# Part of a weight matrix loaded onto half of the partitions, in eight loads of eight partitions each

## The chip, the cores and the metric

The kernel runs on one core of a Trainium2 chip. The metric is device time in microseconds (us), the median of several executions. The profile is of one execution. Its span leaves out 1.5 to 1.9 us that the time includes.

Names used below: PE is TensorE, DVE is VectorE, SP is the queue that issues the loads. A "load" is one DMA from HBM into SBUF. A core has 16 DMA engines, and an ordinary load is divided over all 16 (the trace has 16 completion instants for each).

## The reference, cut to what matters

One token passes through an attention block with a cache of 65,536 positions and then through a gated feed-forward block. The change concerns the last product alone, `w_down` (3584 rows, 7.3 MB).

```python
def _B_ref(x, w_gate, w_up, w_down):          # x: 1 x 1024, F = 3584
    return _gelu(x @ w_gate) * (x @ w_up) @ w_down
...
h = _layernorm(x, axis=-1) * (1 + cb) + sb
x = x + gb * _B_ref(h, B_w_gate, B_w_up, B_w_down)
```

## The kernel before

All weights and the cache are streamed through ten SBUF slots by loads on the SP queue, mostly 2 MiB each. The product with a vector takes each 128x128 piece of the weights as the stationary operand and one column of the vector as the moving one, and waits for one load at a time. So PE works in bursts: it waits for a load, then does that load's matmuls.

```python
def matvec(bank, jobs, rhs, ready, nblk, pick=None, first=True):
    PE.wait(*ready)
    for (jb, view, k0, nk) in jobs:
        PE.wait(jb.tok)                      # this load has landed, on all its engines
        for kk in range(nk):
            for j in range(nblk):
                w = pick(view, kk, j) if pick else view[:, kk, j * P:(j + 1) * P]
                ins = pe.matmul(bank[:, j:j + 1], w, rhs[:, k0 + kk:k0 + kk + 1], ...)
        tok = PE.done(ins)
        release(jb, tok)                     # the slot may be loaded again
...
# w_down: row = (b * 128 + p) * 4 + e lies on partition p; 7 blocks b of 512 rows
wd_v = B_w_down.rearrange("(b p e) n -> p b e n", p=P, e=UE)
while b + 2 < NBF:                           # three loads of two blocks, 2 MiB each
    jb = plan_load(wd_v[:, b:b + 2, :, :], ...)
while b < NBF:                               # the last block as two loads of 512 KiB
    for e in range(0, UE, 2):
        jb = plan_load(wd_v[:, b, e:e + 2, :], flat(2, D), next(tail))
...                                          # (all cut)
v = matvec(acc_bank["dn"], j_d, u_col, (v_uc,), KD)
DVE.wait(v)
v = DVE.done(dve.tensor_tensor(t_dn, acc_bank["dn"], mod_sb[gb], ALU.mult))   # indices cut
# then y = t_dn + x1, a transpose on PE, and the store of 2 KB
```

`t_dn` is the first DVE instruction after the last matmul. Its start is a good mark for the end: what follows it (a sum, a transpose, a cast, a store) takes nearly the same time (2.7 to 2.8 us from its start to the end of the span).

## Time and profile before

| | before |
|---|---|
| time, median of 3 (range) | 444.28 us (444.15 to 444.35) |
| span of the profiled execution | 442.7 us |
| last up load landed on its last engine | 421.6 us |
| third 2 MiB down load, last engine | 436.8 us |
| last load, first and last engine | 433.8 and 439.2 us |
| `t_dn` starts | 439.90 us |

The first fence is from the page of the kernel before: the forty-slice view (busy tenths of the 16 DMA engines, then GB/s moved), the view of DMA queues (packets, MB, share of 16 engines' span), and the chain of waits that ended last.

```profile
DMA  8999999999999999999999999999999999999994
GB/s 329 429 423 426 434 431 426 429 427 421 432 429 432 426 427 437 432 429 428 434 434 430 429 429 433 431 434 429 429 434 431 432 429 428 423 424 424 427 425 177
...
q1 hardware_dynamic: 15328, 185.61, 98.5%
q8 instruction: 25, 0.41, 0.3%
...
DMA 75%; PE 20%; issue 2%; DVE 1%; SPq 1%; ACT 1%
```

The kernel is bound by the DMA engines: their loads (q1) keep them busy for 98.5% of the span. The small line q8: 25 packets of 16 KiB that bring instructions (instruction fetches). They run on the same DMA engines as the loads: one sets the loads of its engine back by 1.41 to 1.42 us (below).

The second fence is the timeline of PE and DVE in the last 20 us before the end: start and duration in us, engine, line, operation, output and inputs, how many, and in brackets the idle time ahead with what ended it.

```profile
421.68 2.03 PE L316 MATMUL kt_ps<-h_col,slot 128*128 128x1 bf16 x56 [2.25 <-DMA slot<-in_B_w_up_dram]
423.81 0.18 DVE L660 SCALAR_TENSOR_TENSOR u_col<-g,kt_ps 128x28 bf16<-128x28 f32 x1 [15.94 <-PE kt_ps L316]
...
426.74 1.84 PE L316 MATMUL kt_ps<-u_col,slot 128*128 128x1 bf16 x64 [3.03 <-DMA slot<-in_B_w_down_dram]
...
431.52 1.87 PE L316 MATMUL kt_ps<-u_col,slot 128*128 128x1 bf16 x64 [2.93 <-DMA slot<-in_B_w_down_dram]
...
436.83 2.29 PE L316 MATMUL kt_ps<-u_col,slot 128*128 128x1 bf16 x80 [3.45 <-DMA slot<-in_B_w_down_dram]
...
439.28 0.58 PE L316 MATMUL kt_ps<-u_col,slot 128*128 128x1 bf16 x16 [0.15 <-DMA slot<-in_B_w_down_dram]
439.90 0.17 DVE L664 TENSOR_TENSOR t_dn<-kt_ps,mod_sb 128x8 f32<-128x8 f32 x1 [15.91 <-PE kt_ps L316]
```

Each burst starts within 0.14 us of its load's landing. The third 2 MiB load (436.83) and the first 512 KiB load give one burst of 80 matmuls, and PE then waits only 0.15 us for the last load.

**Two finer readings of the trace.** They carry the argument, so here is how they are made.

- *Completion counts.* A load's semaphore rises by one for each DMA engine that has finished its share. The trace has these 16 instants for each load, so it shows how far apart the engines are.
- *Following the packets.* The trace has start, duration, size and queue of every packet, but not its engine. One engine's packets follow each other without a gap (the next one is recorded some 3 ns before the end of the last), and each engine has a known number of packets per load. Chaining the packets by these two rules gives 16 streams. It also shows which stream an instruction packet interrupts. Where two streams coincide to 2 ns, the chain may take one for the other.

These are the completion counts of the last load of before (us):

```
433.8 434.0 434.3 434.3 434.4 434.6 435.7 436.6 | 438.0 438.2 438.3 438.7 438.8 438.8 438.8 439.2
```

Eight engines are early, eight are 1.4 to 5.4 us behind them, and the gap is made by the instruction packets. Each takes 0.88 to 1.01 us on one engine, and that engine's loads are set back by more than that. An engine that meets none needs 4.90 us for its share of a 2 MiB down load. They go to eight engines in turn, as far as the chain can be followed.

### The profile page before, as it was taken

How to read it: one execution, taken by the hardware profiler on the slowest of the kernel's cores; microseconds unless marked ns; L12 is line 12 of the kernel's file. 1: busy time of each engine (PE TensorE's matmuls, PEld its weight loads, DVE VectorE, ACT ScalarE, POOL GpSimd, SP SyncE). 2: the span in 40 equal slices, each digit the busy share in tenths (PEclk: the TensorE clock that was granted, in tenths of full speed). 3: DMA queues.
4: the chain of work that ended last, by engine and by line, in shares of the span. 5: the costliest groups of instructions: out<-in, count | busy, mean ns of one | idle time of the engine just before them, and what ended most of it. 6: DMA issues, size and time to landing. Idle time of an engine off the chain costs nothing.

```text
span 442.7 us, 16779 instructions
## 1 busy us (share of the span) xinstructions
PE 335.0 (76%) x7849; PEld 325.2 (73%) x7849; DVE 164.8 (37%) x282; ACT 143.1 (32%) x548; POOL 3.8 (1%) x21
## 2 busy tenths in 40 slices
PE   1333468898979899989899988979898974654434
PEld 1333458898979899979799987969898964654434
DVE  1000046544536445544644644554544443210000
ACT  1000013444444333634533453543343562000000
POOL 2000000000000000000000000000000000000000
PEclk9999999867788956967955996895967785555555
DMA  8999999999999999999999999999999999999994
GB/s 329 429 423 426 434 431 426 429 427 421 432 429 432 426 427 437 432 429 428 434 434 430 429 429 433 431 434 429 429 434 431 432 429 428 423 424 424 427 425 177
DMA packets 15392, 186.08 MB, mean 420 GB/s; under 512 B 1536, under 2 KB 1536, under 8 KB 3840
## 3 DMA queue, kind: packets, MB, share of 16 engines
q1 hardware_dynamic: 15328, 185.61, 98.5%
q8 instruction: 25, 0.41, 0.3%
q14 instruction: 7, 0.06, 0.0%
q10 hardware_dynamic: 32, 0.00, 0.0%
HBM read 185.60 MB, written 0.00 MB: 419 GB/s over the span
## 4 chain that ended last, share of the span: by engine, by line
DMA 75%; PE 20%; issue 2%; DVE 1%; SPq 1%; ACT 1%
DMA slot<-in_A_v_cache_dram 55%; PE kt_ps L417 9%; DMA slot<-in_A_wq_dram 8%; DMA slot<-in_B_w_up_dram 6%; DMA slot<-in_B_w_down_dram 6%; PE b L481 5%; PE sc_ps L437 3%; PE kt_ps L316 1%; SPq L212 1%; PE b L461 1%; ACT p_sb L547 1%; PE b L451 1%; DVE kt_sb L612 0%; PE b L621 0%; DVE zs L597 0%
## 5 line engine op out<-in xcount | busy, mean ns | idle before, releaser
L417 PE MATMUL kt_ps<-ident,slot 128*128 128x128 bf16 x2048 | 171.9, 252 | 4.9 <-DMA slot<-in_A_k_cache_dram 3.0
L516 DVE COPY kt_sb<-kt_ps 128x2048 bf16<-128x2048 bf16 x96 | 117.5, 1225 | 100.0 <-PE kt_ps L417 99.7
L417 PEld LDWEIGHTS kt_ps<-ident,slot 128*128 128x128 bf16 x2048 | 148.6, 114 | 6.6 <-issue 4.2
L516 ACT ACTIVATE kt_sb<-kt_ps 128x2048 bf16<-128x2048 bf16 x32 | 60.1, 1878 | 217.7 <-PE kt_ps L417 217.7
L481 PE MATMUL b<-p_sb,slot 128*128 128x8 bf16 x2048 | 71.0, 167 | 29.5 <-DMA slot<-in_A_v_cache_dram 20.9
L481 PEld LDWEIGHTS b<-p_sb,slot 128*128 128x128 bf16 x2048 | 65.1, 100 | 32.2 <-DMA slot<-in_A_v_cache_dram 22.2
L547 ACT ACTIVATE p_sb<-sc_ps,mneg 128x64 bf16<-128x64 f32 x256 | 83.6, 560 | 5.7 <-DVE mneg L542 5.7
L547 ACT ACTIVATION_READ_ACCUMULATOR p_sb<-sc_ps,mneg 128x1 f32 x256 | 77.2, 364 | 0.0
L437 PE MATMUL sc_ps<-q_buf,kt_sb 128*128 128x8 bf16 x2048 | 67.4, 167 | 0.1
L437 PEld LDWEIGHTS sc_ps<-q_buf,kt_sb 128*128 128x128 bf16 x2048 | 65.1, 100 | 0.2 <-issue 0.2
L316 PE MATMUL kt_ps<-h_col,slot 128*128 128x1 bf16 x448 | 16.2, 172 | 16.9 <-DMA slot<-in_B_w_up_dram 9.1
L316 PEld LDWEIGHTS kt_ps<-h_col,slot 128*128 128x128 bf16 x448 | 15.6, 118 | 17.6 <-DMA slot<-in_B_w_up_dram 9.4
L316 PE MATMUL sc_ps<-s_col,slot 128*128 128x1 bf16 x384 | 11.5, 165 | 15.8 <-DMA slot<-in_w_mod_dram 15.8
L535 DVE TENSOR_REDUCE m_col<-sc_ps 128x8 f32<-128x512 f32 x32 | 21.8, 681 | 4.4 <-PE sc_ps L437 4.4
L316 PEld LDWEIGHTS sc_ps<-s_col,slot 128*128 128x128 bf16 x384 | 11.0, 105 | 16.4 <-DMA slot<-in_w_mod_dram 16.4
L540 DVE TENSOR_REDUCE mg<-b 8x1 f32<-8x128 f32 x32 | 8.9, 279 | 34.4 <-PE b L451 34.4
L316 PE MATMUL sc_ps<-h_col,slot 128*128 128x1 bf16 x256 | 7.4, 165 | 12.6 <-DMA slot<-in_A_wq_dram 12.6
L316 PEld LDWEIGHTS sc_ps<-h_col,slot 128*128 128x128 bf16 x256 | 7.1, 104 | 12.9 <-DMA slot<-in_A_wq_dram 9.3
L461 PE MATMUL b<-negi,mg 8*128 8x8 f32 x64 | 15.0, 304 | 0.4 <-DVE mg L540 0.4
L461 PEld LDWEIGHTS b<-negi,mg 8*128 8x128 f32 x64 | 12.0, 233 | 2.6 <-DVE mg L540 0.6
L316 PE MATMUL kt_ps<-u_col,slot 128*128 128x1 bf16 x224 | 6.6, 165 | 9.6 <-DMA slot<-in_B_w_down_dram 9.6
L316 PEld LDWEIGHTS kt_ps<-u_col,slot 128*128 128x128 bf16 x224 | 6.3, 104 | 9.9 <-DMA slot<-in_B_w_down_dram 6.8
(74 smaller groups left out, 63.2 us busy)
## 6 DMA issues: line engine op xcount, KB each, us to landing
slot<-in_A_k_cache_dram SPq DMA_DIRECT2D x32, 2048.0 KB, 29.6
slot<-in_A_v_cache_dram SPq DMA_DIRECT2D x32, 2048.0 KB, 33.2
slot<-in_w_mod_dram SPq DMA_DIRECT2D x8, 1536.0 KB, 19.0
slot<-in_A_wq_dram SPq DMA_DIRECT2D x4, 2048.0 KB, 37.0
slot<-in_A_wo_dram SPq DMA_DIRECT2D x4, 2048.0 KB, 34.7
slot<-in_B_w_gate_dram SPq DMA_DIRECT2D x4, 1792.0 KB, 39.4
slot<-in_B_w_up_dram SPq DMA_DIRECT2D x4, 1792.0 KB, 29.0
slot<-in_B_w_down_dram SPq DMA_DIRECT2D x3, 2048.0 KB, 30.4
```

Of the source, the lines that this page charges most:

```text
L212: sp.dma_start(j.view, j.src).then_inc(j.tok[0], 16)
L316: ins = pe.matmul(bank[:, j:j + 1], w, rhs[:, k0 + kk:k0 + kk + 1], start=first, stop=True, skip_group_check=True,)
L417: ins = pe.transpose(kt_ps[:, half * 2048 + t * P:half * 2048 + (t + 1) * P], j_k[i].view[:, b * TB + t, :], ident[:, :],)
L437: ins = pe.matmul(sc_ps[:, base + n * REP:base + (n + 1) * REP], kt_sb[:, j % 2, n, :], q_buf[:, j % SITES, :], start=True, stop=True,)
L451: ins = pe.transpose(b6[0:REP, 32:32 + P], m_col[:, j % 2, :], identf[:, :]) if emit else None
L461: ins = pe.matmul(b6[:, 256:256 + REP], mg8[:, j % 2:j % 2 + 1].to_broadcast([REP, P]), negi[:, :], start=True, stop=True,)
L481: ins = pe.matmul(b7[:, s * REP:(s + 1) * REP], j_v[j].view[:, n, :], p_sb[:, s, n, :], start=(n == 0), stop=(n == CH - 1),)
L516: ev[i % SITES][b].done(act.activation(dst, src, ACT.Copy) if E_ is AC else dve.tensor_copy(dst, src))
L535: m1[s].done(dve.tensor_reduce(m_col[:, j % 2, :].unsqueeze(2), scv, AX.X, ALU.max))
L540: m2[s].done(dve.tensor_reduce(mg8[:, j % 2:j % 2 + 1], b6[0:REP, 32:32 + P], AX.X, ALU.max))
L547: ins = act.activation(p_sb[:, s, :, h], scv[:, h, :], ACT.Exp, bias=mneg[:, j, h:h + 1], scale=scale, accum_out=z_all[:, j, h:h + 1],)
```

## The change

The intent is to level the DMA engines. 256 rows of `w_down` (512 KiB) are put on partitions 0 to 63 alone, four rows per partition, and are loaded by eight loads of eight partitions, each four partitions apart. Such a load is divided over eight DMA engines, meant to be the early ones. The other 3328 rows are divided over all 16 as before. Call the eight loads the *low loads*; they come first, then three loads of 2 MiB, then two of 256 KiB (before: three of 2 MiB and two of 512 KiB).

```diff
+HP = 64
+    blocks = [(0, HP, UE), (HP * UE, P, UE // 2)]      # (first row, partitions, rows each)
+    while blocks[-1][0] + blocks[-1][1] * blocks[-1][2] < F:
+        blocks.append((blocks[-1][0] + blocks[-1][1] * blocks[-1][2], P, UE))
+    ucols = [(row0, n, e) for row0, _, n in blocks for e in range(n)]   # 30 columns, were 28
...
+        job.pieces = [(job.view[a], src[a]) for a in parts] if parts else [(job.view, src)]
...
-            sp.dma_start(j.view, j.src).then_inc(j.tok[0], 16)
+            for dst, src in j.pieces:
+                sp.dma_start(dst, src).then_inc(j.tok[0], 16)
...
+        low = [slice(a + t, a + 4 * 8, 4) for a in range(0, HP, 32) for t in range(4)]
+        jb = plan_load(wd_v[0], lambda t: flat(UE, D)(t)[0:HP], next(tail), parts=low)
+        j_d.append((jb, jb.view, ucol0[0], UE))
+        for b in range(2, len(blocks), 2):                 # three loads of 2 MiB
+            ...
+        for e in range(blocks[1][2]):                      # two loads of 256 KiB
+            jb = plan_load(wd_v[1][:, e:e + 1, :], flat(1, D), next(tail))
...
-                            bank[:, j:j + 1], w, rhs[:, k0 + kk:k0 + kk + 1],
+                            bank[:, j:j + 1], w, rhs[0:w.shape[0], k0 + kk:k0 + kk + 1],
```

(Cut to its core; the rest renames sizes.) Because the 64 partitions fill only half a column, the hidden vector needs 30 columns instead of 28: 32 more matmuls for gate and up, 16 more for down.

More of the change, by code (lines that the diff above doesn't have):

```diff
@@ L108, in bass_adaLN_cond__gqa_block_cached__geglu_ffn__decode_kernel @@
     assert FD % UE == 0 and M6 <= SLOT and KD % 2 == 0
+    blocks = [(0, HP, UE), (HP * UE, P, UE // 2)]
+    while blocks[-1][0] + blocks[-1][1] * blocks[-1][2] < F:
+        blocks.append((blocks[-1][0] + blocks[-1][1] * blocks[-1][2], P, UE))
+    assert blocks[-1][0] + P * UE == F and len(blocks) % 2 == 0
+    ucols = [(row0, n, e) for row0, _, n in blocks for e in range(n)]
+    ucol0 = [sum(n for _, _, n in blocks[:i]) for i in range(len(blocks))]
+    FU = len(ucols)
     SP = Eng(nc, nc.sync, "c_sp")
@@ L158, in bass_adaLN_cond__gqa_block_cached__geglu_ffn__decode_kernel @@
     Rmat = kt_sb[:, 0, 0:HQ * HQ // P, :].rearrange("p a b -> p (a b)").rearrange("p (a b) -> p a b", a=HQ)
-    g1 = sb("g1", [P, FD])
-    g2 = sb("g2", [P, FD])
-    g3 = sb("g3", [P, FD])
-    g4 = sb("g4", [P, FD])
-    gth = sb("gth", [P, FD])
-    u_col = sb("u_col", [P, FD], dt.bfloat16)
+    g1 = sb("g1", [P, FU])
+    g2 = sb("g2", [P, FU])
+    g3 = sb("g3", [P, FU])
+    g4 = sb("g4", [P, FU])
+    gth = sb("gth", [P, FU])
+    u_col = sb("u_col", [P, FU], dt.bfloat16)
     t_dn = sb("t_dn", [P, KD])
@@ L184, in bass_adaLN_cond__gqa_block_cached__geglu_ffn__decode_kernel, with plan_load @@
     loads = []
-    def plan_load(src, view_fn, slot, site=None):
+    def plan_load(src, view_fn, slot, site=None, parts=None):
         if site is not None:
@@ L191, in plan_load @@
         else:
-            nfill[slot] += 1
+            nfill[slot] += len(parts or (0,))
             tok = (fill[slot], 16 * nfill[slot])
         job = Job(view_fn(slots[slot]), tok, slot)
-        job.src = src
+        job.pieces = [(job.view[a], src[a]) for a in parts] if parts else [(job.view, src)]
         job.freed = None
@@ L233, in emit_all @@
         wu_v = B_w_up.rearrange("(k p) n -> p k n", p=P)
-        wd_v = B_w_down.rearrange("(b p e) n -> p b e n", p=P, e=UE)
+        wd_v = [B_w_down[r0:r0 + np_ * n, :].rearrange("(p e) d -> p e d", e=n) for r0, np_, n in blocks]
         kh = [A_k_cache[0, g].rearrange("(p n) d -> p n d", p=P) for g in range(Hkv)]
@@ L258, in emit_all @@
         j_d = []
-        NBF = FD // UE
-        b = 0
-        while b + 2 < NBF:
+        low = [slice(a + t, a + 4 * 8, 4) for a in range(0, HP, 32) for t in range(4)]
+        jb = plan_load(wd_v[0], lambda t: flat(UE, D)(t)[0:HP], next(tail), parts=low)
+        j_d.append((jb, jb.view, ucol0[0], UE))
+        for b in range(2, len(blocks), 2):
+            assert blocks[b][0] + P * UE == blocks[b + 1][0]
             jb = plan_load(
-                wd_v[:, b:b + 2, :, :],
+                B_w_down[blocks[b][0]:blocks[b][0] + 2 * P * UE, :].rearrange("(b p e) n -> p b e n", p=P, e=UE),
                 lambda t: t[:, 0:2 * UE * D].rearrange("p (b e n) -> p b e n", b=2, e=UE),
@@ L266, in emit_all @@
             )
-            j_d.append((jb, jb.view.rearrange("p b e n -> p (b e) n"), b * UE, 2 * UE))
-            b += 2
-        while b < NBF:
-            for e in range(0, UE, 2):
-                jb = plan_load(wd_v[:, b, e:e + 2, :], flat(2, D), next(tail))
-                j_d.append((jb, jb.view, b * UE + e, 2))
-            b += 1
+            j_d.append((jb, jb.view.rearrange("p b e n -> p (b e) n"), ucol0[b], 2 * UE))
+        for e in range(blocks[1][2]):
+            jb = plan_load(wd_v[1][:, e:e + 1, :], flat(1, D), next(tail))
+            j_d.append((jb, jb.view, ucol0[1] + e, 1))
         issue_ready()
@@ L639, in pick_gu @@
         def pick_gu(view, kk, j):
-            b, e = divmod(j, UE)
-            return view[:, kk, b * UE * P:(b + 1) * UE * P].rearrange("p (m e) -> p e m", e=UE)[:, e, :]
-        g = acc_bank["g"][:, 0:FD]
-        v_g = matvec(acc_bank["g"], with_view(j_g), h2_col, (v_h2,), FD, pick_gu)
+            row0, n, e = ucols[j]
+            return view[:, kk, row0:row0 + n * P].rearrange("p (m e) -> p e m", e=n)[:, e, :]
+        g = acc_bank["g"][:, 0:FU]
+        v_g = matvec(acc_bank["g"], with_view(j_g), h2_col, (v_h2,), FU, pick_gu)
         DVE.wait(v_g)
@@ L656, in emit_all @@
         v = DVE.done(dve.scalar_tensor_tensor(g2[:, :], gth[:, :], 1.0, g1[:, :], ALU.add, ALU.mult))
-        v_u = matvec(acc_bank["u"], with_view(j_u), h2_col, (v_h2,), FD, pick_gu)
+        v_u = matvec(acc_bank["u"], with_view(j_u), h2_col, (v_h2,), FU, pick_gu)
         DVE.wait(v, v_u)
         v_uc = DVE.done(
-            dve.scalar_tensor_tensor(u_col[:, :], g2[:, :], 0.5, acc_bank["u"][:, 0:FD], ALU.mult, ALU.mult)
+            dve.scalar_tensor_tensor(u_col[:, :], g2[:, :], 0.5, acc_bank["u"][:, 0:FU], ALU.mult, ALU.mult)
         )
```

## The prediction

> **What bounds the kernel now.** DMA. The forty-slice view has the 16 DMA engines at nine tenths in nearly every slice; the queue view gives the load queue 98.5% of their span; the chain of waits is 75% DMA. In the trace's packet records a 16 KiB packet takes 611 ns and an engine starts its next about 607 ns later: each engine runs at a fixed 27 GB/s, and the end is set by the engine with most work.
>
> The engines do not end together. Each load's completion count climbs by one per DMA engine, and the trace has these 16 instants. In the last load (512 KiB) they are 433.8, 434.0, 434.3, 434.3, 434.4, 434.6, 435.7, 436.6 us for eight engines and 438.0 to 439.2 for the others. After it come its 16 matmuls (to 439.86), result, transpose and store, to 442.7. The lag is made by instruction fetches: 25 packets of 16 KiB on the instruction queue, each 0.88 to 1.01 us on one engine. Following the packet times, each sets one engine back about 1.2 us, and only eight engines get them, in turn. The eight-partition loads of x and c (8 packets each) interleave with the other eight. [...]
>
> **What the change does.** [...] Late engines lose 32 KiB, 1.21 us; early ones gain 1.21 us[...]. Early ends become 435.1 to 437.9, late ones 436.8 to 438.0: nearly level. The last two loads shrink to 256 KiB. Added: 32 matmuls for gate and up (60 instead of 56 per load; 36 ns each) and 16 for down (28.6 ns each), mostly under loads; eight more DMA issues of about 0.35 us, ahead of need (the last load was issued near 416 us, moved from 432).
>
> **On the critical path.** The late engines carry the same bytes up to the third 2 MiB load, so that still lands at about 436.8 us. Before, 80 matmuls then ran to 439.12 and waited 0.15 us for the last load's 16. After, the two small loads land near 437.4 and 438.0, while PE needs until 436.83 + 2.29 = 439.12 for the 80 matmuls left. Of the 1.2 us that DMA gains, about 0.5 is lost to TensorE's tail: the end comes 0.7 us earlier.
>
> **Prediction: 443.6 us, range 442.9 to 444.4.** Faster by over 2%: 1%; within 2%: 98%; slower by over 2%: 1%.
>
> **What would show it.** The last load's final count near 438.0, its spread 2 to 3 us instead of 5.4; the third 2 MiB load still near 436.8; 80 down matmuls with no DMA wait before the last ones; t_dn near 439.2; the low loads landing before the last up load is consumed (about 424).
>
> **What would make it wrong.** The 48 extra matmuls move instruction fetches earlier: a fetch that now meets a late engine before 436.8 costs up to 1.2 us, and eats the gain. If the low loads use the late engines, the end is 1.2 us later (445). If eight small DMAs cost queue room, the last loads start late. A chip difference of a few tenths is of the gain's size.

In the prediction is a rule that numbers the engines of a small load, and a length for completion packets. The rule led from "interleave with the other eight" to low loads on the eight early engines, which would get 64 KiB each where all 16 had 32. The sum for the end: 1.2 us gained by DMA, less 0.5 for TensorE's tail, makes 0.7, and 444.3 becomes 443.6. Of the early ends, 435.1 to 437.9, a term is 0.1 us (433.8 and 436.6 plus 1.21 make 435.0 and 437.8); they are not in that sum. The completion packets take 9 ns in the traces.

## The result, and the profile after

The changed kernel took 445.44 us, median of five runs (445.11 to 446.96), against 444.28 us before (444.04 to 444.35). The ratio of times is 1.0035 with a 95% interval of 1.0023 to 1.0047. Ratios here are the mean time of one kernel's runs over that of the other's of the same rounds, so they are not quite the ratio of the medians quoted. So it is within 2%, but clearly slower, by 1.2 us, where a gain of 0.7 us had been predicted, and it lies outside the predicted range (442.9 to 444.4).

The page of the changed kernel, same views as above:

```profile
DMA  8999999999999999999999999999999999999993
GB/s 327 428 427 425 430 430 435 427 424 424 429 432 427 433 428 432 433 430 432 430 435 425 435 429 435 427 432 429 438 427 432 428 435 429 421 423 424 428 419 156
...
q1 hardware_dynamic: 15456, 185.61, 98.4%
q8 instruction: 25, 0.41, 0.3%
...
DMA 79%; PE 17%; issue 1%; ACT 1%; DVE 1%; SPq 1%
```

Nothing in the averages tells the two kernels apart: the same bytes, the same rate, as many instruction packets. The last slices differ, and the timeline shows them (L325 is the line that was L316):

```profile
421.96 2.13 PE L325 MATMUL kt_ps<-h_col,slot 128*128 128x1 bf16 x60 [2.17 <-DMA slot<-in_B_w_up_dram]
424.44 1.01 PE L325 MATMUL kt_ps<-u_col,slot 64*128 64x1 bf16 x32 [0.35 <-DVE u_col L669]
428.44 1.86 PE L325 MATMUL kt_ps<-u_col,slot 128*128 128x1 bf16 x64 [2.99 <-DMA slot<-in_B_w_down_dram]
433.33 1.86 PE L325 MATMUL kt_ps<-u_col,slot 128*128 128x1 bf16 x64 [3.03 <-DMA slot<-in_B_w_down_dram]
438.22 2.29 PE L325 MATMUL kt_ps<-u_col,slot 128*128 128x1 bf16 x80 [3.03 <-DMA slot<-in_B_w_down_dram]
...
440.55 0.17 DVE L673 TENSOR_TENSOR t_dn<-kt_ps,mod_sb 128x8 f32<-128x8 f32 x1 [16.17 <-PE kt_ps L325]
```

The first 2 MiB load lands at 428.44 instead of 426.74, and the third at 438.22 instead of 436.83. The 80 matmuls behind it run without a wait, as predicted, and set the end: `t_dn` at 440.55 instead of 439.90. So the loss is in the landing of the 2 MiB loads, which the prediction had left where they were.

The completion counts of the last load show who is late (us):

```
433.2 433.4 435.2 435.2 435.2 435.7 437.1 437.3 437.5 437.6 437.7 437.9 437.9 438.1 | 439.3 439.5
```

Fourteen engines are done by 438.1, as predicted for all 16. Two are more than 1 us behind them. Following the packets through the trace says which. Below, per stream: the instruction packets that met it from 352 us on (start, us), its low packets, and the start of its completion packets for the last up load and the last load (us; the count that PE sees is 0.3 to 0.5 us later).

```
changed kernel                                    before
fetches     low  last up   last load              fetches     last up   last load
-            8   416.30    434.79                 -           416.35    433.55
-            8   416.41    434.90                 -           416.47    433.67
-            8   416.45    434.94                 -           416.77    433.96
-            8   416.90    435.39                 -           416.77    433.96
-            8   418.29    436.77                 -           416.91    434.10
-            8   418.91    437.40                 -           417.03    434.23
396          8   420.63    439.12   <--           -           418.23    435.42
404          8   420.49    438.97   <--           -           419.10    436.30
-            0   416.83    432.82                 395         420.63    437.83   <--
-            0   417.06    433.06                 404         420.50    437.70   <--
428          0   419.83    437.24                 432         420.24    438.86
390          0   420.98    436.97                 389         420.86    438.05
421          0   420.18    437.59                 422         419.85    438.46
413          0   421.27    437.26                 413         421.23    438.43
371          0   421.59    437.59                 370         421.35    438.55
384          0   421.63    437.62                 383         421.29    438.49
```

The eight engines that move the low loads and the eight that get the instruction packets are not disjoint. They share two (marked; in this trace the fourth and the fifth of the round, though streams that coincided earlier may be swapped). Those two were late already and now carry 64 KiB of these rows where they had carried 32. And two early engines carry no low load and idle from 433.1 on.

The last instruction packet of each trace (437.6 and 439.4 us) is left out of the table: streams were ending or had ended then, so which one met it can't be told, and no load was set back by it. A second chaining had to give every stream whole loads in their order; it gives the same 16 streams for both kernels, and agrees with what is told of experiments 1 and 8.

### The profile page after: what moved, and what is told of

Read it like the earlier page. It is cut to its first block, busy times and chain, and to the rows that moved or that the text cites. A ratio compares the mean times of both kernels' runs of the same rounds, so it can differ in the third digit from the quotient of the medians.

```text
span 443.3 us, 16883 instructions
## 1 busy us (share of the span) xinstructions
PE 335.6 (76%) x7897; PEld 325.7 (73%) x7897; DVE 164.8 (37%) x282; ACT 143.2 (32%) x548; POOL 3.8 (1%) x21
## 4 chain that ended last, share of the span: by engine, by line
DMA 79%; PE 17%; issue 1%; ACT 1%; DVE 1%; SPq 1%
DMA slot<-in_A_v_cache_dram 52%; PE kt_ps L426 8%; DMA slot<-in_A_k_cache_dram 8%; DMA slot<-in_B_w_up_dram 8%; DMA slot<-in_B_w_down_dram 6%; DMA slot<-in_w_mod_dram 5%; PE b L490 4%; PE sc_ps L446 3%; PE kt_ps L325 1%; SPq L222 1%; ACT p_sb L556 1%; PE b L470 1%; PE b L460 0%; ACT kt_sb L525 0%; DVE kt_sb L525 0%
## 5 line engine op out<-in xcount | busy, mean ns | idle before, releaser
L325 PE MATMUL kt_ps<-h_col,slot 128*128 128x1 bf16 x480 | 17.1, 172 | 16.1 <-DMA slot<-in_B_w_up_dram 8.7
L325 PEld LDWEIGHTS kt_ps<-h_col,slot 128*128 128x128 bf16 x480 | 16.4, 117 | 16.8 <-DMA slot<-in_B_w_up_dram 9.0
L325 PE MATMUL sc_ps<-s_col,slot 128*128 128x1 bf16 x384 | 11.5, 165 | 16.1 <-DMA slot<-in_w_mod_dram 16.1
L325 PEld LDWEIGHTS sc_ps<-s_col,slot 128*128 128x128 bf16 x384 | 11.1, 105 | 16.7 <-DMA slot<-in_w_mod_dram 16.7
L325 PE MATMUL sc_ps<-h_col,slot 128*128 128x1 bf16 x256 | 7.5, 165 | 12.5 <-DMA slot<-in_A_wq_dram 12.5
L325 PEld LDWEIGHTS sc_ps<-h_col,slot 128*128 128x128 bf16 x256 | 7.1, 104 | 12.8 <-DMA slot<-in_A_wq_dram 9.3
L325 PE MATMUL kt_ps<-u_col,slot 128*128 128x1 bf16 (+1 forms) x240 | 7.0, 165 | 9.4 <-DMA slot<-in_B_w_down_dram 9.1
L325 PEld LDWEIGHTS kt_ps<-u_col,slot 128*128 128x128 bf16 (+1 forms) x240 | 6.7, 104 | 9.7 <-DMA slot<-in_B_w_down_dram 9.3
```

Source lines behind the costliest of these rows:

```text
L325: ins = pe.matmul(bank[:, j:j + 1], w, rhs[0:w.shape[0], k0 + kk:k0 + kk + 1], start=first, stop=True, skip_group_check=True,)
```

## The experiments

Three theories were put against each other. **A**: two of the engines that get instruction packets are among those that move the low loads. **B**: the 48 extra matmuls are more instructions, and bring an instruction packet that falls in a bad place. **C**: the eight small loads cost their engines time beyond their bytes.

### 1. The changed kernel again (label again)

No edit.

> The changed kernel once more, to see how its runs spread. Theory A (two of the eight engines that get the instruction fetches are among the eight that move the low loads): of the 16 counts of the first 2 MiB down load, less those of the last up load, two late engines again show 7.4 us and two early ones 4.9 us; the last load lands 439.3 to 439.5 us with two engines over 1 us behind the other six late ones. Time 445 to 447, over before by 0.8 to 2.7 us, with more spread than before's 0.3 us. Theory B (the 48 extra matmuls bring one more instruction fetch in time to delay one engine): one engine, not two, is behind, and which one changes.

Measured: 445.58 us median (445.3 to 446.0, four runs) against 444.18 before, ratio 1.0035 (1.0019 to 1.0052). The last load's counts end with 438.1, 438.2 | 439.5, 439.6: two engines behind. Following the packets gives the same picture as above: six low-load streams reach the end of the up loads between 416.3 and 418.5, and two, both interrupted by instruction packets, at 420.7. This agrees with A. B had one engine behind.

C falls with these traces too. A low-load stream goes from the completion of the up load to that of its eighth low load in 2.50 us (416.30 to 418.80), and eight packets of 8 KiB at 309 ns take 2.44 us once their overlap of some 3 ns is taken off. So a small load costs its engine about 7 ns beyond its bytes, and the six early ones among the eight are never last.

### 2. The low rows in one load over all engines (label all16)

```diff
-        low = [slice(a + t, a + 4 * 8, 4) for a in range(0, HP, 32) for t in range(4)]
+        low = None
```

> The low 256 rows in one DMA of 64 partitions, so over all 16 engines, 32 KiB each, as many bytes per engine as before; the extra matmuls, the split and the small last loads stay. Theory A: every late engine is as late as in before, the third 2 MiB load lands near 438.0 (436.8 and 1.2 us), the last load near 439.2 with a spread of 5.4 us, 80 matmuls follow from 438.0, t_dn near 440.4, time near 444.8: 0.4 to 0.6 over before, and under the changed kernel by 0.2 to 1 us. Theory B: the third 2 MiB load lands as late or later than in the changed kernel by another 1.2 us (439.4), time 446.5. Theory C (eight small DMAs cost time on their engines beyond their bytes): as A in time, but then the low-load engines of the changed kernel would all be late by the same, which its counts must show.

Measured: 449.34 us against 444.18 before, ratio 1.0118 (1.0101 to 1.0135). This missed all three expectations, those of A and C by 4.5 us and that of B by 2.8 us, because the experiment was not the clean control it was meant to be. The load of 64 partitions kept all 16 engines busy (DMA share 1.02 below), but from 422 to 426 us all its packets of 8 KiB are slow, with medians of 545 ns in the first two of these microseconds and 616 in the last two, instead of 309, and the up packets beside them are slowed too (481 instead of 272 ns). The windows view of 416 to 427 us, of this kernel and then of the changed one (busy time of each engine, granted clock, DMA share, GB/s), shows it in sum:

```profile
416.00:427.00 11.00, 4.27 (x120) 4.10 (x120) 0.16 (x1) 0.00 (x0) 0.00 (x0) 0.50 1.02 269
```

```profile
416.00:427.00 11.00, 5.27 (x152) 5.02 (x152) 0.18 (x1) 0.00 (x0) 0.00 (x0) 0.50 1.01 425
```

The engines are as busy (1.02), yet move 269 instead of 425 GB/s. So a full "busy" share does not mean full speed: the same packets take longer. What slows them is not shown; the trace shows only that they are slow. The change's own low loads, of eight partitions four apart, do not have this fault: in its trace, from 416 to 428 us, only one 8 KiB packet is over 309 ns (804, in the wake of an instruction packet). This run is 5.2 us over before, where experiment 5, whose first load has as many bytes on all 128 partitions, is 0.5 over. It says nothing on A against B.

### 3 and 4. Marking the engines (labels marks and marks2)

The trace has no engine numbers, but loads of few partitions use few engines (the 64 low packets of the changed kernel lie on eight streams, eight on each). The author assumed that a smaller load uses a part of the engines of a larger one. Then low loads of different sizes give each engine, or pair of engines, its own number of low packets: pairs of 13, 9, 6 and 4 in the first run, and 11, 11, 10, 8, 8, 6, 6 and 4 in the second.

```diff
-        low = [slice(a + t, a + 4 * 8, 4) for a in range(0, HP, 32) for t in range(4)]
+        low = [slice(t, 32, 4) for t in range(4)]                                # 4 of eight
+        low += [slice(32 + t, 32 + 4 * 6, 4) for t in (0, 1)]                    # 2 of six
+        low += [slice(34, 48, 4), slice(35, 48, 4), slice(50, 64, 4)]            # 3 of four
+        low += [slice(56, 64, 4), slice(57, 64, 4), slice(51, 56, 4), slice(59, 64, 4)]
```

> The same 64 partitions of low rows in loads of eight, six, four and two partitions (4, 2, 3 and 4 loads)[...]. Each packet with its completion is about 0.32 us, so the offsets between the counts of the last up load and of the first 2 MiB down load are 4.9 us plus 4.1, 2.9, 1.9, 1.3 and 0. Theory A: exactly two late engines show one of the offsets over 0, and its size tells which pair they belong to. If all eight late ones show 4.9 us, theory A is wrong. Time about 446 to 448, not of interest.

Measured: 445.94 us, one run. The packet counts that follow from the assumption came out: two streams each with 13, 9, 6 and 4 low packets, eight with none. Two late streams had low packets: one with 4, one with 6. Both had met instruction packets.

The second one splits the pairs (loads of eight, five, three, seven and two):

```diff
+        low = [slice(t, 32, 4) for t in range(4)]
+        low += [s for t in (0, 1) for s in (slice(32 + t, 52, 4), slice(52 + t, 64, 4))]
+        low += [slice(32 + t, 60, 4) for t in (2, 3)] + [slice(62, 64, 1)]
```

> The low partitions in loads of eight (4), five and three (2 of each), seven (2) and two (1)[...]. In the runs so far, following the packet times gave two engines that get instruction fetches and carry low packets, in the run of marks with 6 and 4 low packets[...]. Theory A expects two such engines again[...]. If no fetch engine carries low packets here, theory A is wrong.

Measured: 445.3 us, one run, on another chip. Again two streams with instruction packets (at 397 and 404) carry low loads. One has 6 low packets. Of the other, the chain follows three and loses the rest; 61 of the 64 low packets are assigned, so the three that remain are its own, which makes 6. The second chaining assigns all 64 and gives 6 to both, and 6 and 4 in the first run. On the same assumption an engine with 6 in the first run has 8 or 6 here, and one with 4 has 6 or 4, so six and six fits. Which engines of the core the two are is not shown; that two engines are in both sets is. A stands.

### 5. The order alone, no engine favoured (label even2)

The first 512 rows as two blocks of two rows on all 128 partitions. Order and small last loads stay, the extra matmuls go.

```diff
-    blocks = [(0, HP, UE), (HP * UE, P, UE // 2)]
+    blocks = [(0, P, UE // 2), (P * UE // 2, P, UE // 2)]
...
-        jb = plan_load(wd_v[0], lambda t: flat(UE, D)(t)[0:HP], next(tail), parts=low)
+        jb = plan_load(wd_v[0], flat(UE // 2, D), next(tail))
```

> The first 512 rows as two blocks of two rows on all 128 partitions: no engine gets more than another,[...] the matmuls are as many as before; the order and the two small last loads stay as in the changed kernel. Theory A and the tail of TensorE: third 2 MiB load at 438.0, last load at 439.2 with a spread of 5.4 us, 80 matmuls from 438.0 to 440.3, t_dn 440.4 (before 439.9), time 444.7 (+0.4 to +0.6). Theory B (the extra matmuls' fetches are the loss): like before, 444.2. Theory C (small DMAs): 443.6 to 444.2, as nothing small is left in front.

Measured: 444.52 us (444.39 to 444.58) against 444.05 before (443.89 to 444.14). The ratio 1.0011 has an interval that includes 1 (0.9994 to 1.0027), but the runs of the two do not overlap. Timeline of its end:

```profile
437.59 2.29 PE L324 MATMUL kt_ps<-u_col,slot 128*128 128x1 bf16 x80 [3.00 <-DMA slot<-in_B_w_down_dram]
...
439.92 0.17 DVE L672 TENSOR_TENSOR t_dn<-kt_ps,mod_sb 128x8 f32<-128x8 f32 x1 [16.06 <-PE kt_ps L324]
```

The last load landed at 438.8, but 80 matmuls from 437.59 on were still running, and `t_dn` came 1.1 us after the landing, where before needs 0.7 (439.2 to 439.90). By the medians the new order alone costs about 0.5 us. The trace offers a reason: 256 KiB land in 0.65 us each, less than PE needs to catch up with the 2 MiB load before them, so PE ends 0.4 us later after the landing. This is the term that the prediction called PE's tail, and its size fits. But the loss itself is not in this trace, whose `t_dn` is no later than that of before (439.92 and 439.90), because the landings were 0.4 us earlier; the traces vary by that much. That the order costs 0.5 us is thus likely and not proven.

### 6. PE's tail in the changed kernel (label after_split)

```diff
         for b in range(2, len(blocks), 2):
+            if b + 2 == len(blocks):                  # the third 2 MiB as two of 1 MiB
+                for bb in (b, b + 1):
+                    jb = plan_load(wd_v[bb], flat(UE, D), next(tail))
+                    j_d.append((jb, jb.view, ucol0[bb], UE))
+                continue
```

> The changed kernel with its third 2 MiB load cut into two of 1 MiB, so that TensorE has 48 instead of 80 matmuls left when the last big load lands. If TensorE's tail is worth what the trace says (32 matmuls, 0.9 us, less what the last load's own landing then limits): landings as in the changed kernel (438.2 for the last 1 MiB, 439.5 for the last load), t_dn 439.9 instead of 440.55, time 0.5 to 0.8 under the changed kernel, so 444.8 to 445.0. If the tail doesn't bound the end: no change, 445.5.

Measured: 444.59 us (444.44 to 444.69) against 444.05 before, ratio 1.0011 (0.9995 to 1.0028). It is 0.54 us over before, where the changed kernel was 1.2 and 1.4 us over before in its two sets of rounds, so the cut is worth 0.6 to 0.9 us by medians of different chips, and 0.4 us between the two traces.

```profile
438.42 1.67 PE L330 MATMUL kt_ps<-u_col,slot 128*128 128x1 bf16 x48 [1.43 <-DMA slot<-in_B_w_down_dram]
...
440.12 0.17 DVE L678 TENSOR_TENSOR t_dn<-kt_ps,mod_sb 128x8 f32<-128x8 f32 x1 [16.20 <-PE kt_ps L330]
```

The last big load lands as late as in the changed kernel (438.4), so the two overloaded engines are still there (last load: 437.6 | 439.3, 439.7), but 48 matmuls are left instead of 80, and `t_dn` starts at 440.12 instead of 440.55.

### 7 and 8. The same idea with engines that are all early (labels four and four_al)

128 rows, eight per partition, on partitions 0 to 15, in four loads of four partitions, meant for four early engines without the two shared ones (four streams carry these packets in experiment 8). The last 2 MiB load is cut as in 6. The expectation's figure for the last load, 438.6, is 439.2 less 0.6: the twelve other engines lose 16 KiB each, 0.6 us at the 607 ns that an engine takes for 16 KiB in before.

```diff
-HP = 64
+HP = 16
+LE = 8
...
+    blocks = [(0, HP, LE), (HP * LE, P, UE - HP * LE // P)]
...
+        low = [slice(t, HP, 4) for t in range(4)]
```

> The same idea with the two late engines left out: 128 rows, eight per partition, on partitions 0 to 15, in four loads of four partitions[...]; half the bytes; the last 2 MiB cut as above, then three small loads. Theory A:[...] no low-load engine is the last; last load 438.6, t_dn 439.0, time 443.4. But the 168 extra matmuls bring the next instruction fetch from 439 to about 432, which may set one late engine back by 1.2 us: last load 439.2 to 439.8, time 444.0 to 444.5. If the identity of the engines is not the cause, it is no better than the changed kernel with the same cut (444.9).

Measured: 448.53 us against 444.05, ratio 1.0101 (1.0085 to 1.0118), 3.6 us or more over every expectation. The cause is not in the last stage. Its last up load landed at 425.2 us, 3.6 us later than in before, and the packets were longer in all stages: 16 KiB packets took 615.9 ns on average from 60 to 340 us, against 612.0 in before, and 7 KiB packets 277.3 against 273.1 from 390 to 415 us. The edit had done one more thing. With 35 columns, the small tensors that are allocated ahead of the load slots need more room, and the slots began at byte 62,400 of a partition instead of 62,208. The first is 192 over a multiple of 256, the second is a multiple of 256. Two runs test that. The first repeats *four* with 64 bytes of padding (slots at 62,464, a multiple of 256):

```diff
     y_row = sb("y_row", [KD, P], dt.bfloat16)
+    pad = sb("pad", [P, 16])
```

> The kernel 'four' with 64 bytes of padding, so that the load slots begin at a multiple of 256 bytes again, as in before (in 'four' they began 192 bytes past one; its packets took 274 instead of 272 and 616 to 622 instead of 611 ns in all stages, and the last up load landed 3.6 us later than in before). If that is the cause: packets at 272 and 611 ns again, last up load near 421.6,[...] time 444.2 to 444.6; one engine over 1 us behind the rest by the fetch near 431.6, and no low-load engine last. If the loss came from loads of four engines: 448.

Measured: 444.74 us (444.37 to 444.84) against 444.18, ratio 1.0008 (0.9991 to 1.0025). The packets are back at 612.0 and 273.4 ns, and the last up load landed at 421.8. So the 3.8 us were the address. The version gains nothing over before, and its trace says why:

```profile
437.92 1.62 PE L332 MATMUL kt_ps<-u_col,slot 128*128 128x1 bf16 x48 [1.42 <-DMA slot<-in_B_w_down_dram]
439.78 0.38 PE L332 MATMUL kt_ps<-u_col,slot 128*128 128x1 bf16 x8 [0.24 <-DMA slot<-in_B_w_down_dram]
```

The last load's counts are 433.4 to 438.4 for 15 engines and 439.7 for one. The chain of packets finds four streams with four low packets each, none of them with an instruction packet, and none last. The one that is last is a late engine that met an instruction packet at 371 and a second one at 431: the 168 extra matmuls had brought the next round of instruction packets 8 us forward. So A holds here too, with the two shared engines taken out, and what B described is real in this version, though not in the changed kernel. There the packet after the eighth of the round came at 437.6 us and delayed no load: fourteen engines were done by 438.1, and the two others needed 0.65 us for each of the last two loads, as the rest did. That the idea would pay with neither fault, the shared engines and the early packet, was not tested.

### 9. The slots 64 bytes further, nothing else (label before_shift)

The padding above in the kernel before, so that its slots begin at 62,272, 64 over a multiple of 256.

> The kernel before with 64 bytes of padding ahead of the load slots and nothing else, so that they begin 64 bytes past a multiple of 256. If the address is what slowed 'four': 16 KiB packets 616 to 622 instead of 611 ns, every stage slower by about 0.8%, time 447.5 to 448.5. If not: 444.2.

Measured: 448.15 us (448.03 to 448.29) against 444.18, ratio 1.0088 (1.0071 to 1.0105). The line of GB/s over the forty slices, to be held against that of before:

```profile
GB/s 333 423 423 419 427 429 424 420 428 421 426 423 430 427 427 429 429 427 427 430 429 428 426 430 425 430 427 430 426 430 427 425 430 429 416 417 418 420 417 175
```

All slices between the first and the last had 421 to 437 GB/s and now have 416 to 430, and 16 KiB packets average 615.9 ns. A tensor of 64 bytes that nothing uses costs 4 us. Only these starts were run, 0, 64 and 192 over a multiple of 256, and that the step is 256 is not shown: both fast starts, 62,208 and 62,464, are multiples of 128 too, and neither slow one is. The changed kernel did not have this fault: its slots begin at 62,208, as before.

### 10. One more instruction packet, the loads untouched (label before_fetch)

126 idle matmuls between the gate and up loads of the kernel before, where PE waits anyway (1.3 to 2.3 us for each of these loads in before).

```diff
                 tok = PE.done(ins)
+                for _ in range(extra if jb is not jobs[-1][0] else 0):      # extra = 21, six times
+                    pe.matmul(b7[:, 256:257], ident[:, :], rhs[:, 0:1], start=True, stop=True)
                 release(jb, tok)
```

> The kernel before with 126 idle matmuls on TensorE between the gate and up loads (their result is not used; PE waits 2 us per load there), and nothing changed in the loads: 252 more instructions, nearly one 16 KiB instruction fetch. If a fetch sets one DMA engine back by 1.2 us and the last engine sets the end: the fetch that before has at 439.4 now comes near 432, falls on the engine that got the one at 370 (near 438.8 at the end), which then ends near 440.0; last load 439.7 to 440.0 instead of 439.2, t_dn 440.3 to 440.7, time 444.6 to 445.0 (+0.4 to +0.9). If fetches don't matter: no change (within 0.2).

Measured: 445.21 us (444.89 to 445.7) against 444.18, ratio 1.0019 (1.0002 to 1.0036). The view of DMA queues and the end of the timeline:

```profile
q8 instruction: 26, 0.43, 0.3%
```

```profile
437.97 2.29 PE L316 MATMUL kt_ps<-u_col,slot 128*128 128x1 bf16 x80 [4.25 <-DMA slot<-in_B_w_down_dram]
440.42 0.59 PE L316 MATMUL kt_ps<-u_col,slot 128*128 128x1 bf16 x16 [0.15 <-DMA slot<-in_B_w_down_dram]
441.04 0.17 DVE L666 TENSOR_TENSOR t_dn<-kt_ps,mod_sb 128x8 f32<-128x8 f32 x1 [16.64 <-PE kt_ps L316]
```

One more instruction packet (26), at 431.8 us, put one engine at 440.4 and left the other 15 at 439.2 or earlier. The third 2 MiB load lands 1.1 us later than in before, `t_dn` is 1.1 us later, and the median rises by 1.0 us, a little over what was expected (the ratio, by means, says 0.8, with an interval from 0.1 to 1.6). This execution was the slowest of the four. Another one of the same kernel was profiled too: there the packet came at 431.5 us, on the engine that had met the one at 371, that engine ended at 440.0 and the rest by 438.8, and `t_dn` was at 440.68, 0.8 us later than in before. This shows the mechanism alone: one instruction packet on one late engine near the end costs the whole kernel about 1 us. The 252 more instructions (17,031 instead of 16,779) brought one more packet of 16 KiB, as expected.

### 11 and 12. A version without balancing (labels before_split and split5)

The kernel before with smaller loads at its end: the third 2 MiB load as two of 1 MiB, the last block as four of 256 KiB.

```diff
-        while b + 2 < NBF:
+        while b + 3 < NBF:
...
-            for e in range(0, UE, 2):
-                jb = plan_load(wd_v[:, b, e:e + 2, :], flat(2, D), next(tail))
+            n = 1 if b + 1 == NBF else UE
+            for e in range(0, UE, n):
+                jb = plan_load(wd_v[:, b, e:e + n, :], flat(n, D), next(tail))
```

> The kernel before with smaller loads at the end alone: the third 2 MiB load as two of 1 MiB, the two of 512 KiB as four of 256 KiB, no balancing. The last load lands as in before, 439.2 or 439.3, but only 8 instead of 16 matmuls follow it: t_dn 439.65 instead of 439.90, time 0.2 to 0.3 under before, less if the fetches fall otherwise. A version that should beat both.

Measured: 443.88 us (443.84 to 444.09) against 444.18, ratio 0.9991 (0.9975 to 1.0008): the right size, but inside the interval. So it was run again with five rounds:

> The version 'before_split' once more with five rounds, as its gain of 0.3 us (443.88 against 444.18) was inside the interval of three. If the gain is that of TensorE's shorter tail: 443.8 to 444.0 against 444.1 to 444.3, ratio 0.9990 to 0.9996, all its runs under nearly all of before. If it was chance: ratio 0.9998 to 1.0003.

Measured: 444.09 us (443.93 to 444.53) against 444.12, ratio 0.9999 (0.9985 to 1.0012). The gain is not confirmed. The tail of PE is shorter in both traces (`t_dn` 0.45 us after the last landing instead of 0.7), but the last load landed at 439.0 in the first and at 439.5 in the second. The engines' phases move by half a microsecond from run to run, more than the tail is worth. No version is shown to beat the kernel before.

## Why the prediction was wrong

- **The bound, the rate, eight early and eight late engines: right.** The 1.2 us by which an instruction packet sets its engine back was too small; the traces give 1.41 to 1.42. Experiment 10 shows the cost of such a packet by itself. The rate, 16 KiB in 607 ns, is that of these two kernels; packets took longer in experiments 2, 7 and 9 (545 and 616 instead of 309 ns, and 615.9 instead of 612.0).
- **"The eight-partition loads of x and c (8 packets each) interleave with the other eight": the step from this to the eight early engines failed.** That eight engines get the instruction packets is right, and that eight engines move an eight-partition load is right. But it was concluded that the two sets are complements, and they share two. The chain of packets made for the prediction had in fact given two streams with both kinds of packets, but it could confuse streams, and the two were put down to that. Counting the packets of each load in the chain would have settled it beforehand.
- **"The late engines carry the same bytes up to the third 2 MiB load, so that still lands at about 436.8 us": false for the two.** In before they ended their share of that load 1.0 to 1.2 us ahead of the last engine. The low loads add 2.5 us to them there. The load landed at 438.22 us, 1.4 later.
- **Late ends of "436.8 to 438.0": right for six of eight.** All engines outside the two were done by 438.1. The two ended at 439.3 and 439.5, after every engine of before.
- **80 matmuls in one burst: right; 0.5 us lost to PE's tail: fits** (experiment 5: 0.5 us by medians, with an interval that includes none; experiment 6: the cut gives 0.4 us back between traces and 0.6 to 0.9 by medians). It made the error visible at once, since the end follows the third load and not the last one.
- **The sum.** Predicted `t_dn` 439.2, found 440.55: 1.35 of the 1.84 us between 443.6 and 445.44. Of the rest, 0.33 us is that the profiled execution was the fastest of the five (445.11), and 0.16 is that the time was 4.56 us over `t_dn` there, where 4.4 was reckoned. Against before, `t_dn` is 0.65 us later and the median 1.16, so the trace shows a little over half of the measured loss; the rest is in spread and in time outside the span, and not explained. That the changed kernel spreads over 1.9 us, where before spreads over 0.3, is not explained: no trace of a slower execution was at hand.
- **The risks that the prediction named.** "If the low loads use the late engines, the end is 1.2 us later (445)" is what happened, for two engines of the eight; it was named as a risk, but the sum did not count on it. Another, extra matmuls that move an instruction packet, did not strike here, but did in experiments 7 and 8, with 168 extra matmuls. Queue room: the last load was issued at 418.1 us instead of 414.5, still 13 us before the first packet of the last two loads (431.5). Chips: the medians of before in the sets of rounds lie between 444.05 and 444.28 us.

## What to carry to other kernels

To level DMA engines, first prove which engines are late: mark them with loads of different numbers of partitions and count the packets of each stream. Two wrong engines among eight made this balancing move a loss of 1.2 us, since a load has landed only when its last engine is done (PE starts within 0.14 us of that). Instruction packets use the same DMA engines as the data, so more code can slow a DMA-bound kernel: 252 more instructions brought one more packet near the end and cost about 1 us (experiment 10). When an edit changes the size of any tensor, look at the addresses of those allocated after it, or the experiment measures that instead (64 bytes cost 4 us in experiment 9).
